# Loading a weight megabyte behind the first keys, with a new issue list for the repeated pass

## The chip, the core and the metric

The kernel runs on one core of a Trainium2 chip. Its engines work from queues of their own, each in the order in which its instructions were written: TensorE (PE, with PEld for its weight loads), VectorE (DVE), ScalarE (ACT), GpSimd (POOL), and SyncE (SP), which here only issues DMAs. The metric is the device time of one execution in microseconds, the median over several executions.

## The reference

Eight batches, 8 heads, 576 positions, head dimension 64. Keys and values are averaged over groups of 8 positions, softmax attention runs over the 72 pooled positions, and a gated block follows:

```python
scores = scale * np.matmul(q, k_p.transpose(0, 1, 3, 2))      # k_p: mean of 8 keys
attn = softmax(scores); x = attn @ v_p                        # heads side by side: [8, 576, 512]
h = gelu(x @ w_in)                                            # w_in [512, 1024], 8-byte numbers
u, v = h[..., :512], h[..., 512:]
v_n = (v - mean(v)) / sqrt(var(v) + 1e-6) * g_ln
v_s = einsum('ts,bsd->btd', w_sg, v_n) + b_sg                 # w_sg [576, 576]
out = x + (u * v_s) @ w_out
```

## The kernel before

The work of a batch is cut into steps, each a Python generator that issues some instructions and stops; each stop waits for its next turn. An entry `S3+1` in a list gives one more turn to step S, part 3, of the batch one ahead of the current one; a lower-case entry is work on weights (`lv0` loads a megabyte of the value half of w_in, `v0` gives a turn to the rebuilding of its first 128 rows, `d0` issues two matmuls on a block of zeros). Four lists are played: PROLOGUE (batch 0 and the weights), FIRST (around batch 1), PERIOD (played five times, for batches 2 to 6) and LAST (batch 7). All engines take their order from them, and nothing reorders it afterwards. An entry whose step is already finished issues nothing.

The steps that matter here, with their lines:

- A, B, C, E load keys, values, queries and the last eight pooled positions of a batch ("left"). `load` is line 222, and all of these go to SP's queue. SP has eight semaphores for its DMAs and uses them in turn, so its ninth DMA waits until the first has landed, the tenth for the second, and so on.
- `v0`, `v1` turn the 8-byte numbers of w_in into 4-byte ones: two ACT instructions (lines 263 and 267), two DVE (269, 270), one POOL (272), then a rounded part by ACT (275) and a rest by POOL (277).
- K pools the keys. In batch 0 PE does it (tiles kvraw and bbc), ACT copies the result (tile kp, 419), DVE pools the left positions (lp, 407), PE transposes kp and lp (445, 447), and ACT writes the scaled key block kbd (459, 460).
- Q transposes the queries (530) and ACT copies them into qbuf (533). S multiplies qbuf by kbd for the scores (a group of kbd,qbuf matmuls), DVE finds the maxima (557), ACT the exponentials (576; in batch 0, 571), DVE the reciprocals (593, 594) and the product (597).
- s transposes w_sg in five pieces (303), each split by ACT (225, 310) and DVE (227, 312).
- H is the value half of x @ w_in (5 parts), with normalisation on DVE (762, 763, 768) and POOL (765, 766). U is the other half, W the multiplication by w_sg (matmuls wsh,vk), with DVE (833, 835) behind it. V, G and O are attention times values, sums for a seven-product multiplication, and the product with w_out. P pools the values (vp, 407).

PSUM is four double banks that are handed around in the order in which they were given back. A step that takes a bank waits for the last reader of the step that gave that bank back.

Of the kernel before, what the change touches and what calls it, by code (L numbers as in the profile page):

```python
# [20 lines left out]


PROLOGUE = """
d0 lv0 d0 A1+0 A0+0 E0+0 v0 d0 E1+0 C0+0 d0 d0 v1 v0 C1+0 K2+0 d0 d0 v1 d0 K1+0 K1+0 K0+0 K0+0 K2+0 P2+0 Q0+0 K2+0
Q1+0 Q0+0 S0+0 v0 S0+0 C2+0 S0+0 Q2+0 Q1+0 v0 v1 lv1 v1 S1+0 S1+0 v0 C3+0 Q2+0 S2+0 S1+0 S2+0 v1 ls0 S0+0 Q3+0 S0+0
B0+0 B1+0 S1+0 Q3+0 S2+0 S0+0 A1+1 S0+0 S2+0 S3+0 S1+0 v3 s2 S2+0 S0+0 S0+0 T0+0 s2 T0+0 S3+0 S2+0 v3 S1+0 s1 S3+0
S1+0 v3 S2+0 s0 S3+0 s4 s2 S1+0 s1 s4 S3+0 s1 S3+0 A0+1 lu0 S3+0 s0 v2 S1+0 v3 S2+0 S3+0 P1+0 E0+1 s4 S2+0 s0 T1+0
# [20 lines left out]
O0+0 S2+0 Z3+0 Z0+0 Z2+0 Z3+0 V3+1 Z2+0  # L48
""".split()
PERIOD = """  # L50
V1+0 S0+1 S0+1 S0+1 H3+0 H3+0 H3+0 V0+0 H1+0 H2+0 V3+0 H0+0 H1+0 H1+0 H3+0 H2+0 H2+0 S1+1 H3+0 H1+0 V2+0 U0+0 H0+0
H1+0 H2+0 S1+1 H0+0 Q2+1 H2+0 H4+0 S1+1 C3+1 H0+0 Q3+1 H4+0 S1+1 U1+0 H0+0 H4+0 S3+1 H3+0 U0+0 S3+1 T0+1 H0+0 H4+0
H4+0 U1+0 S3+1 S2+1 P1+1 H4+0 T0+1 S1+1 C2+2 U3+0 A1+2 H1+0 T0+1 S2+1 H4+0 W0-4 S3+1 H2+0 P0+1 S2+1 H4+0 T0+1 S3+1
S2+1 W0+0 S2+1 T0+1 P2+1 W3+0 C0+2 A0+2 P2+1 L0+1 U3+0 P2+1 W0+0 P2+1 K1+2 W1+0 K0+2 U2+0 W1+0 L0+1 G0+0 W2+0 U2+0
W3+0 G1+0 T1+1 G1+0 L0+1 G0+0 L0+1 G1+0 L0+1 Q0+2 W2+0 T2+1 V0+1 G2+0 L0+1 O1+0 T1+1 T1+1 V1+1 E0+2 G2+0 V0+1 B0+2
G4+0 G2+0 T2+1 O0+0 K2+2 T2+1 V2+1 O0+0 G3+0 G2+0 V1+1 T3+1 G2+0 G3+0 W1-5 O0+0 G3+0 T3+1 V2+1 T3+1 V3+1 O0+0 B1+2
O0+0 G4+0 K2+2 O0+0 G4+0 O2+0 V0+1 O1+0 G4+0 K2+2 K2+2 C1+2 O1+0 O2+0 O1+0 K2+2 G4+0 S0+2 Z1+0 Z0+0 O0+0 S0+2 Z1+0
O0+0 Z3+0 V3+1 V1+1 Z0+0 V2+1 Q1+2 Z3+0 Z2+0 Z2+0 V3+1
""".split()
LAST = """  # L60
H1+0 H3+0 V2+0 V1+0 H1+0 H3+0 H1+0 H1+0 H2+0 H3+0 T3-7 H2+0 V0+0 H1+0 H2+0 H0+0 S0-2 V3+0 H4+0 H3+0 H4+0 H3+0 H2+0
# [1009 lines left out]
```

## Time and profile before

| | us |
|---|---|
| median of 3 runs (lowest, highest) | 556.76 (556.32, 559.84) |
| profiled execution | 555.78 |
| its span, first to last instruction | 553.8 |
| TensorE busy in the span | 540.8 |
| VectorE, ScalarE, GpSimd busy | 393.7, 375.9, 358.9 |

The profiled execution is 1.98 us longer than its span, and 0.98 us below the median of the runs. TensorE's granted clock is 0.999 of the full one over the span. Times inside the span are counted from its first instruction; the five passes over PERIOD lie between about 161 and 482 us.

### The profile page before, as it was taken

The numbers are of one execution on the slowest core, as the hardware profiler recorded it, in microseconds if no ns is written. First come the engines' busy times: TensorE is split into PE (matmuls) and PEld (weight loads), VectorE is DVE, ScalarE is ACT, GpSimd is POOL, SyncE is SP. The second block draws the span as 40 slices with busy tenths as digits, with TensorE's granted clock in tenths as the row PEclk, the third lists the DMA queues.
The fourth block names the chain that finished last, engine by engine and source line by source line (L and its number), as shares of the span: only waits on it lengthen the run. The fifth ranks groups of instructions, "written<-read, shape, count | busy, mean of one in ns | idle before, by whom it ended". The sixth has DMA issues, their size and how long they took to land.

```text
span 553.8 us, 10591 instructions
## 1 busy us (share of the span) xinstructions
PE 540.8 (98%) x3665; PEld 505.8 (91%) x3665; DVE 393.7 (71%) x562; ACT 375.9 (68%) x986; POOL 358.9 (65%) x415
## 2 busy tenths in 40 slices
PE   8899999999999999999999999999999999999996
PEld 7688799988999899989999899998999899998996
DVE  5999999767646778567976779567886677455164
ACT  4699658986274897678866696866966798643220
POOL 5578786988788257944589246963489437892440
PEclk9999999999999999999999999999999999999999
DMA  9989723672341644444552725436362530004005
GB/s 249 335 193 255 215 53 71 129 138 45 78 82 18 119 91 127 79 68 83 131 117 35 128 44 136 99 57 118 82 161 39 90 61 12 12 14 73 1 1 86
DMA packets 204197, 54.33 MB, mean 98 GB/s; under 512 B 185904, under 2 KB 191664, under 8 KB 204144
## 3 DMA queue, kind: packets, MB, share of 16 engines
q1 hardware_dynamic: 199280, 53.07, 45.1%
q10 hardware_dynamic: 4864, 0.59, 0.7%
q8 instruction: 29, 0.48, 0.4%
q14 instruction: 24, 0.20, 0.1%
HBM read 40.21 MB, written 13.42 MB: 97 GB/s over the span
## 4 chain that ended last, share of the span: by engine, by line
PE 79%; DVE 8%; DMA 4%; ACT 3%; issue 2%; POOL 2%; SPq 1%; DVEq 0%; POOLq 0%; ACTq 0%
PE ps L134 78%; DMA left<-in_moe_w_sg 2%; SPq L222 1%; DVE xmem L921 1%; PE ps L170 1%; DMA kvraw<-in_k 1%; DVE al L689 1%; DMA far<-e 1%; DVE ps L833 1%; DVE umem L835 1%; ACT ah L682 1%; ACT gk L849 1%; PE ps L303 0%; DVE e L567 0%; DVE vp L407 0%
## 5 line engine op out<-in xcount | busy, mean ns | idle before, releaser
L134 PE MATMUL ps<-wsh,vk 128*128 128x288 f32 x512 | 97.1, 296 | 0.1
L134 PE MATMUL ps<-xhlk,wih 128*128 128x288 f32 x512 | 90.3, 298 | 1.5 <-DVE e L597 0.7
L134 PE MATMUL ps<-wih,xhlk 128*128 128x512 f32 x256 | 83.5, 398 | 0.3 <-DVE e L597 0.2
L134 PEld LDWEIGHTS ps<-wsh,vk 128*128 128x128 f32 x512 | 78.2, 188 | 1.3 <-DVE left L768 1.3
L134 PEld LDWEIGHTS ps<-xhlk,wih 128*128 128x128 f32 x512 | 75.4, 188 | 3.2 <-PE ps L134 0.9
L576 ACT ACTIVATE e<-ps,nmax 128x72 f32<-128x72 f32 x240 | 73.0, 336 | 6.5 <-DVE nmax L557 2.5
L134 PEld LDWEIGHTS ps<-wih,xhlk 128*128 128x128 f32 x256 | 48.1, 188 | 12.2 <-DVE e L597 0.5
L134 PE MATMUL ps<-wsl,vk 128*128 128x288 f32 x256 | 57.4, 295 | 0.0
L134 PE MATMUL ps<-xhlk,wil 128*128 128x288 f32 x256 | 55.1, 296 | 0.0
L576 ACT ACTIVATION_READ_ACCUMULATOR e<-ps,nmax 128x1 f32 x240 | 53.4, 223 | 0.0
L134 PE MATMUL ps<-wil,xhlk 128*128 128x512 f32 x128 | 50.6, 395 | 0.0
L774 POOL TENSOR_TENSOR vk<-xmem,vk 128x512 fp32r<-128x512 f32 x32 | 40.9, 1290 | 14.6 <-ACT vk L772 14.5
L605 POOL COPY el<-e 128x40 f32<-128x40 f32 x64 | 12.8, 254 | 53.8 <-issue 22.3
L921 DVE TENSOR_TENSOR xmem<-ps,xmem 128x576 f32<-128x576 f32 x42 | 31.5, 751 | 22.8 <-PE ps L134 22.4
L721 POOL TENSOR_TENSOR xhlk<-xmem,xhlk 128x576 fp32r<-128x576 f32 x32 | 45.2, 1434 | 1.4 <-ACT xhlk L719 1.4
L134 PE MATMUL ps<-gk,woh 128*128 128x288 f32 x224 | 46.1, 297 | 0.0
L134 PE MATMUL ps<-kbd,qbuf 128*128 128x144 f32 x320 | 44.2, 288 | 1.5 <-ACT qbuf L533 1.0
L134 PEld LDWEIGHTS ps<-kbd,qbuf 128*128 128x128 f32 x320 | 41.4, 190 | 3.7 <-ACT qbuf L533 1.4
L134 PEld LDWEIGHTS ps<-wsl,vk 128*128 128x128 f32 x256 | 42.2, 188 | 0.0
L134 PEld LDWEIGHTS ps<-xhlk,wil 128*128 128x128 f32 x256 | 41.0, 188 | 0.0
L865 POOL TENSOR_TENSOR umem<-umem 128x576 f32<-128x576 f32 x24 | 34.4, 1432 | 8.2 <-issue 6.9
L833 DVE SCALAR_TENSOR_TENSOR ps<-ps,gcol,bbc 128x576 f32<-128x576 f32 x28 | 22.9, 820 | 22.5 <-PE ps L134 22.3
(198 smaller groups left out, 1424.3 us busy)
## 6 DMA issues: line engine op xcount, KB each, us to landing
kvraw<-in_k SPq DMA_DIRECT2D x32, 256.0 KB
qbuf<-in_q SPq DMA_DIRECT2D x112, 72.0 KB
out<-umem SPq DMA_DIRECT2D x112, 72.0 KB
kvraw<-in_v SPq DMA_DIRECT2D x28, 256.0 KB
vraw<-in_moe_w_in SPq DMA_DIRECT2D x2, 1024.0 KB
graw<-in_moe_w_in SPq DMA_DIRECT2D x2, 1024.0 KB
eraw<-far SPq DMA_DIRECT2D x28, 72.0 KB
far<-e SPq DMA_DIRECT2D x7, 256.0 KB
```

Source lines behind the costliest of these rows:

```text
L134: nc.tensor.matmul(o, lhsT, rhs, start=start, stop=stop, **flags)
L170: nc.tensor.transpose(ps[:rows, i * P:(i + 1) * P], src(i), ident if i < NT - 1 else swap)
L222: queue.dma_start(o, i)
L576: nc.scalar.activation(e[:, i, h], slots[i][:, h], AF.Exp, bias=nmax[:, i, h:h + 1], **acc)
L605: nc.gpsimd.tensor_copy(st["el", b].rearrange("p t (n j a) -> p t n j a", n=2, a=4)[:, :, g // 2, :, 2 * (g % 2) + h], ef[:, :, LEFT[h]:LE ...
L682: nc.scalar.copy(ah, ps[:, 0:S])
L689: nc.vector.tensor_tensor(al, ps[:, 0:S], ah.bitcast(F32), op=ALU.subtract)
L721: nc.gpsimd.tensor_tensor(xhl[:, 1, g], x32[:, g], xhl[:, 0, g].bitcast(F32), op=ALU.subtract)
L774: nc.gpsimd.tensor_tensor(lo, vg, hi.bitcast(F32), op=ALU.subtract)
L833: nc.vector.scalar_tensor_tensor(vs, vs, gcol[:, d:d + 1], bbc.rearrange("p (a n) -> p a n", a=2), op0=ALU.mult, op1=ALU.add)
L865: nc.gpsimd.tensor_tensor(x, p, q, op=ALU.subtract)
L921: nc.vector.tensor_tensor(x, ps[:, :, 0:HALF], x, op=ALU.add)
```

## The change

In PROLOGUE the entry `lv0` moves from the second place to behind `A1+0 A0+0`, the loads of the keys of batch 0. The entries of PERIOD are the same 172 as before in another order. FIRST, LAST and the rest of PROLOGUE are not touched, and no instruction is added or removed.

```diff
 PROLOGUE = """
-d0 lv0 d0 A1+0 A0+0 E0+0 v0 d0 E1+0 C0+0 d0 d0 v1 v0 C1+0 K2+0 d0 d0 v1 d0 K1+0 K1+0 K0+0 K0+0 K2+0 P2+0 Q0+0 K2+0
+d0 d0 A1+0 A0+0 lv0 E0+0 v0 d0 E1+0 C0+0 d0 d0 v1 v0 C1+0 K2+0 d0 d0 v1 d0 K1+0 K1+0 K0+0 K0+0 K2+0 P2+0 Q0+0 K2+0
...
 PERIOD = """
-V1+0 S0+1 S0+1 S0+1 H3+0 H3+0 H3+0 V0+0 H1+0 H2+0 V3+0 H0+0 H1+0 H1+0 H3+0 H2+0 H2+0 S1+1 H3+0 H1+0 V2+0 U0+0 H0+0
...
+H2+0 S0+1 H3+0 V3+0 H1+0 H2+0 V1+0 S0+1 H3+0 H2+0 V0+0 H1+0 H3+0 V2+0 H0+0 H2+0 H1+0 H3+0 C3+1 S1+1 H4+0 H1+0 H2+0
...
```

SP's queue at the start of the program is the one place where the first edit shows; the other four engines keep their order up to the first pass over PERIOD. Here kvraw<-in_k are the keys of batch 0, vraw the megabyte of w_in, and left the last eight positions:

```order
 L1067 UNCONDITIONAL_BRANCH
+L222 DMA kvraw<-in_k 128x1x512 x4
 L222 DMA vraw<-in_moe_w_in 128x2x1024
-L222 DMA kvraw<-in_k 128x1x512 x4
 L222 DMA left<-in_k 32x1x512 x2
 L222 DMA left<-in_v 32x1x512 x2
```

The four DMAs of keys pass the one of w_in; what follows keeps its place.

DVE in the second pass over PERIOD, from the maxima of the third set of scores (S3) on, before. ps_3047 and ps_3081 are the banks of S3 and S2, ps_2989 that of H4, the last part of H:

```order
L557 TENSOR_REDUCE nmax_3055<-ps_3047 128x10
L762 BN_STATS bst_3061<-ps_2989 64x6
L763 BN_AGGR mv_3062<-bst_3061 64x2
L407 TENSOR_REDUCE vp_3087<-kvraw_2731 128x128
L768 TENSOR_SCALAR left_120<-ps_2989,mv_3062,rstd_3065 64x512
L665 STREAM_TRANSPOSE eraw_110<-eraw_110 128x576
L557 TENSOR_REDUCE nmax_3130<-ps_3081 128x10
L593 TENSOR_SCALAR ps_3047<-ssum_3070 128x5x2
L594 RECIPROCAL ps_3047<-ps_3047 128x5x2
L597 TENSOR_TENSOR e_3069<-e_3069,ps_3047 128x720
L407 TENSOR_REDUCE vp_3087<-kvraw_2657 128x128
```

And the same stretch in the change, where ps_3061 is the bank of S3, ps_3076 that of S2 and ps_2950 that of H4:

```order
L557 TENSOR_REDUCE nmax_3067<-ps_3061 128x10
L762 BN_STATS bst_3069<-ps_2950 64x6
L763 BN_AGGR mv_3070<-bst_3069 64x2
L768 TENSOR_SCALAR left_120<-ps_2950,mv_3070,rstd_3073 64x512
L539 STREAM_TRANSPOSE qbuf_111<-qbuf_111 128x576
L557 TENSOR_REDUCE nmax_3085<-ps_3076 128x10
L407 TENSOR_REDUCE vp_2995<-kvraw_2757 128x128
L593 TENSOR_SCALAR ps_3061<-ssum_3088 128x5x2
L594 RECIPROCAL ps_3061<-ps_3061 128x5x2
L597 TENSOR_TENSOR e_3087<-e_3087,ps_3061 128x720
```

The pooling of the values (L407) that stood ahead of H4's last reader (L768) now stands ahead of the reciprocals of S3; of the other moves on DVE, a query transposition (L539) comes forward and the transposition of eraw (L665) goes back. On PE, H4 passes the first U, and the W parts come in the order 1, 0, 3, 2 where they came as 0, 3, 1, 2. The first W takes H4's bank and the second W S3's bank, before and after.

## Rows read from the trace of the kernel before

**Rows 1.** The page: span, TensorE's busy time, DMA rate in 40 slices.
```profile
span 553.8 us, 10591 instructions
...
PE 540.8 (98%) x3665; PEld 505.8 (91%) x3665; DVE 393.7 (71%) x562; ACT 375.9 (68%) x986; POOL 358.9 (65%) x415
...
GB/s 249 335 193 255 215 53 71 129 138 45 78 82 18 119 91 127 79 68 83 131 117 35 128 44 136 99 57 118 82 161 39 90 61 12 12 14 73 1 1 86
```

**Rows 2.** Stretches: start:end, length, each engine's busy time, clock, DMA share, GB/s.
```profile
290.00:353.90 63.90, 63.78 (x435) 60.14 (x435) 47.43 (x66) 48.16 (x139) 40.57 (x46) 1.00 0.47 93
```

**Rows 3.** SP's issues in order of time: start, us, DMA, count.
```profile
0.73 0.46 SPq L222 DMA_DIRECT2D vraw<-in_moe_w_in  x1
1.25 2.62 SPq L222 DMA_DIRECT2D kvraw<-in_k  x4
```

**Rows 4.** Chain of work that ended last, at the start: start, us, what.
```profile
3.27 6.04 DMA kvraw<-in_k
...
15.17 8.45 DMA left<-in_moe_w_sg
```

**Rows 5.** TensorE in order of time: start, us, group, [idle before, releaser].
```profile
7.53 3.94 PE L134 MATMUL ps<-kvraw,bbc 128*128 128x128 f32 x32
...
12.09 0.27 PE L447 MATMUL ps<-ident,lp 128*128 128x128 f32 x1
...
14.05 1.49 PE L134 MATMUL ps<-kbd,qbuf 128*128 128x144 f32 x10
```

**Rows 6.** ScalarE in order of time.
```profile
5.68 0.67 ACT L263 ACTIVATE tops<-vraw 128x512 f32<-128x512 f32 x1 [3.67 <-DMA vraw<-in_moe_w_in]
...
7.40 0.66 ACT L267 ACTIVATE vraw<-vraw 128x512 int32<-128x512 uint32 x1
...
11.50 0.27 ACT L419 COPY kp<-ps 128x128 f32<-128x128 f32 x1 [1.72 <-PE ps L134]
12.40 0.38 ACT L459 ACTIVATE kbd<-ps 64x256 f32<-64x256 f32 x1 [0.64 <-PE ps L447]
```

**Rows 7.** VectorE in order of time.
```profile
6.38 0.43 DVE L269 TENSOR_SCALAR tops<-tops 128x512 int32<-128x512 int32 x1 [3.64 <-ACT tops L263]
6.84 0.69 DVE L270 SCALAR_TENSOR_TENSOR tops<-vraw,tops 128x512 int32<-128x512 int32 x1
...
9.45 1.93 DVE L407 TENSOR_REDUCE lp<-left 32x128 f32<-32x1024 f32 x1 [1.92 <-DMA left<-in_k]
...
15.58 0.91 DVE L557 TENSOR_REDUCE nmax<-ps 128x10 f32<-128x720 f32 x1 [0.47 <-PE ps L134]
...
41.64 0.91 DVE L557 TENSOR_REDUCE nmax<-ps 128x10 f32<-128x720 f32 x1 [1.35 <-PE ps L134]
```

**Rows 8.** All engines in order of time, around 29 us.
```profile
29.46 0.20 PEld L303 LDWEIGHTS ps<-ident,umem 128*128 128x128 f32 x2 [0.15 <-DVE wtl L312]
```

**Rows 9.** VectorE in order of time, in one pass over PERIOD.
```profile
328.97 1.98 DVE L407 TENSOR_REDUCE vp<-kvraw 128x128 f32<-128x1024 f32 x1
330.88 0.79 DVE L768 TENSOR_SCALAR left<-ps,mv,rstd 64x512 f32<-64x512 f32 x1
331.59 0.76 DVE L665 STREAM_TRANSPOSE eraw<-eraw 128x576 f32<-128x576 f32 x1
332.29 0.86 DVE L557 TENSOR_REDUCE nmax<-ps 128x10 f32<-128x720 f32 x1
...
333.52 0.90 DVE L597 TENSOR_TENSOR e<-e,ps 128x720 f32<-128x720 f32 x1
334.34 2.02 DVE L407 TENSOR_REDUCE vp<-kvraw 128x128 f32<-128x1024 f32 x1
```

**Rows 10.** GpSimd in the same pass.
```profile
329.38 0.54 POOL L766 TENSOR_TENSOR rstd<-rstd,mhalf 64x1 f32<-64x1 f32 x1
```

**Rows 11.** TensorE's weight loads in the same pass.
```profile
331.72 0.30 PEld L134 LDWEIGHTS ps<-wsh,vk 128*128 128x128 f32 x2 [0.25 <-DVE left L768]
...
335.43 0.33 PEld L134 LDWEIGHTS ps<-wsh,vk 128*128 128x128 f32 x2
```

More of the change, by code (lines that the diff above doesn't have):

```diff
@@ L50 @@
 PERIOD = """
-V1+0 S0+1 S0+1 S0+1 H3+0 H3+0 H3+0 V0+0 H1+0 H2+0 V3+0 H0+0 H1+0 H1+0 H3+0 H2+0 H2+0 S1+1 H3+0 H1+0 V2+0 U0+0 H0+0
[L52 to L58, printed above, removed]
+H2+0 S0+1 H3+0 V3+0 H1+0 H2+0 V1+0 S0+1 H3+0 H2+0 V0+0 H1+0 H3+0 V2+0 H0+0 H2+0 H1+0 H3+0 C3+1 S1+1 H4+0 H1+0 H2+0
+W1-5 H0+0 S1+1 S0+1 C0+2 H0+0 Q3+1 H3+0 H1+0 S1+1 H3+0 W0-4 H0+0 P1+1 U1+0 H2+0 H0+0 S1+1 H4+0 H0+0 H4+0 U0+0 T0+1
+U1+0 H4+0 Q2+1 U0+0 S3+1 S3+1 H4+0 S2+1 H4+0 H1+0 Q0+2 S2+1 S3+1 H4+0 P0+1 T0+1 S2+1 H4+0 A1+2 U3+0 S3+1 T0+1 U3+0
+W1+0 S1+1 S2+1 S3+1 A0+2 K1+2 P2+1 S2+1 C2+2 W0+0 P2+1 W0+0 W3+0 T0+1 L0+1 W1+0 K0+2 U2+0 W3+0 G0+0 T0+1 G1+0 P2+1
+G0+0 W2+0 U2+0 P2+1 G1+0 L0+1 L0+1 E0+2 G1+0 L0+1 T2+1 W2+0 L0+1 G2+0 T1+1 V0+1 O0+0 T1+1 C1+2 V0+1 T1+1 L0+1 G2+0
+V1+1 K2+2 G2+0 G4+0 T2+1 G3+0 G2+0 T2+1 O1+0 V1+1 G2+0 O0+0 G3+0 V2+1 T3+1 O0+0 T3+1 G3+0 T3+1 G4+0 O0+0 K2+2 V3+1
+B1+2 K2+2 O0+0 G4+0 O0+0 V2+1 B0+2 O1+0 V3+1 K2+2 V1+1 G4+0 K2+2 O2+0 O2+0 G4+0 O1+0 O1+0 V0+1 S0+2 V2+1 Z1+0 V3+1
+Z1+0 S0+2 Z0+0 O0+0 Q1+2 Z0+0 O0+0 Z3+0 Z2+0 Z3+0 Z2+0
 """.split()
```

## The prediction

> **What bounds the kernel now.** I read the page first: TensorE is busy for 540.8 of 553.8 us, 98% [rows 1]. Only 13.0 us of the span are without a matmul, which is the most that a change of order alone could give back. The stretch table says where they are not: in one pass over PERIOD TensorE is busy for 63.78 of 63.90 us while VectorE has 47.43, ScalarE 48.16 and GpSimd 40.57 [rows 2]. A pass is bound by TensorE's own instructions, and a new order of the same instructions can win tenths of a microsecond in it. It can lose more, because every step hands on one of four PSUM banks and each of the other engines works in order.
>
> The start is bound by something else. The chain of waits begins with SP's issues and the landing of the keys at 9.31 (3.27 + 6.04), goes through SP's next issues, and ends on the landing of the last piece of w_sg at 23.62 [rows 4]. On TensorE, though, the pooling of the keys starts at 7.53 with no idle time before it, straight behind the matmuls on zeros, and runs for 3.94 us in one piece [rows 5]. VectorE is what I followed next: from its first maximum at 15.58 to 41.6 its timeline shows no wait worth listing; the next is 1.35 us at 41.64, for TensorE [rows 7]. And TensorE waits for VectorE at 29.46, when a bank comes free behind a subtraction of w_sg [rows 8]. So whatever makes VectorE late at 15.58 arrives at TensorE at 29.46, and from there TensorE is the one that is late.
>
> **First edit: the megabyte behind the keys.** It removes and adds nothing; five DMAs change places on SP's queue. Four issues of keys take 2.62 us together, so they go from 0.73 to 3.35 instead of 1.25 to 3.87 [rows 3], and the weight issue of 0.46 ends at 3.8. Nothing behind them on SP moves in order, and the lanes that the later issues wait for are the same in number.
>
> *What the keys gain.* Nothing that I can price above 0.1 us: their pooling on TensorE starts at 7.53 behind the matmuls on zeros, which wait for no load, and shows no idle time [rows 5].
>
> *What the weights lose.* They landed just before 5.68, where ScalarE takes them up after 3.67 us of waiting [rows 6]. Now they are the last of the same two megabytes. The last of those two landed at 9.31 [rows 4], with its issue ending at 3.87; the weights' issue would end at 3.8. I take 9.31. The lower bound is 2.1 MB at the second slice's 335 GB/s [rows 1], 6.3 us from 1.2, so 7.5. The row of the same queue with the same bytes ahead is the nearer one.
>
> *Who is queued behind them.* ScalarE: `v0` and `v1` are four instructions, of which the first starts at 5.68 and the last at 7.40 and takes 0.66 [rows 6], so 2.38 us for all. They would run from 9.33 to 11.71, and the two copies of the pooled keys, 0.27 each, follow: the second ends at some 12.2 instead of 11.77. VectorE: lines 269 and 270 of `v0` stand ahead of the pooling of the left keys (lp). Line 269 starts with the end of ScalarE's first instruction, 9.33 + 0.67 = 10.0; line 270 comes 0.46 later and takes 0.69 [rows 7], so lp starts at 11.2 where it started at 9.45. It is 1.75 us late, and ends at 13.1.
>
> *Who waits for that.* TensorE's transposition of lp, at 12.09 [rows 5], moves to 13.15; kbd, which ScalarE begins at 12.40 when that is done [rows 6], is 1.05 late, and so are the first scores, which now begin at 15.1 and end at 16.6. VectorE has its own work in between and had 0.47 us of idle time before its first maximum [rows 7]; that absorbs a part: 1.75 - 0.47 = 1.28 us. The maximum comes at 16.86, behind both. From there nothing on VectorE gives before 41.6, and TensorE takes it over at 29.46. **Term: +1.3 us**, between 0 (weights landed by 7.5: 7.5 + 1.9 = 9.4, when the left keys land anyway) and +1.75 (nothing absorbed). Less than nothing is excluded but for the 0.1 above, since w_sg, the next to be waited for, lands behind the same bytes as before.
>
> **Second edit: the order in PERIOD.** Its end is nearly the same list (two places where VectorE's results are just in time keep their order on all engines), and in its first half the margins are above 0.3 us as I add them up. What changes is the handover to the four W steps. Before, the first W waits 0.25 us for H4's bank [rows 11], because VectorE pools values (1.98 us) ahead of H4's last reader, at 330.88 [rows 9]. GpSimd's factor for that reader is there at 329.92 [rows 10]. In the change it follows at once: 329.95, so the bank is free at 330.7 and the first W doesn't wait. **-0.25 us.** But the second W takes S3's bank, and its last reader (line 597) now stands behind a query transposition, the maxima of S2 and the other pooling of values. With the rows' steps [rows 9]: 329.95 + 0.71 (line 768) + 0.70 (a transposition, by the one at 331.59) + 1.23 (maxima and the two small ones, 332.29 to 333.52) + 2.02 = 334.61, and 0.90 for the product: 335.51. Unhindered the second W would now load its weights at 335.43 - 0.25 = 335.18 [rows 11], so it waits 0.33 us. The two cancel within 0.1 us; I take **0** for each of five passes, with bounds of -0.25 (no second wait) and +0.25 (the second wait half a microsecond), so -1.3 to +1.3 for all. The moved query transposition needs its load, and the moved loads wait on SP for S1's matmuls, but these lie ten microseconds ahead; the eraw transposition that goes back is read 15 us later. I cost both at nothing; if one of them came late, VectorE would hold S3's bank, which is a rival below.
>
> **The sum.** 555.78 for the profiled execution, + 1.3 + 0 = 557.1; by the median of the runs, 556.76 + 1.3 = 558.06, so **558.0**.
>
> **Rivals.** *The weights land early.* The transfers ahead of them may pack better with keys first. The first megabyte alone needed 0.73 to 5.66, 4.93 us; the same from an issue at 3.35 ends at 8.3, lp starts at 10.2, 0.75 late, of which 0.47 are absorbed: +0.3, time 557.0. For it: the DMA rate rises from 249 to 335 GB/s in the second slice [rows 1]. Against it: the keys, as last of the two megabytes, needed until 9.31. In the Trainium skill, "DMA: Bandwidth & Descriptors" (Anatomy of one DMA) gives a fixed 2.0 us plus the bytes at 436 GB/s for one DMA of GpSimd's path; by that, as an estimate, a megabyte issued at 3.4 lands at 7.8 and the term is 0, time 556.8. The 4.93 us measured here for a lone first megabyte is longer than its 4.4.
>
> *The new list is better than my sum.* The first W's wait goes and the second has none: -1.3 over five passes, with the first term 557 - 0.2 = 556.8, without it 555.5. For it: the wait of 0.25 stands in the trace; against it: VectorE's order as written.
>
> *VectorE is held in every pass: slower.* The pooling of values that ran at 334.34 [rows 9] now runs at 332.6, ahead of S3's reciprocals. If its load, or the query load in front of it, is not there, VectorE stands, S3's bank stays taken and TensorE waits from 335.2 on, microsecond for microsecond, five times. Held for 1.1 us more than I add up it costs 1%; at 1.5 us, 7.5 us in all, time 565.5. For it: the reciprocals lose their place ahead of a 2 us reduction. Against it: before, that reduction shows no wait either, and VectorE has 16 us to spare in a pass [rows 2].
>
> **How the numbers follow.** Forecast 0.48; weights early 0.25; list better 0.18; VectorE held 0.07; a gain of over 1%, 5.6 us, would need nearly half of all idle time of TensorE, 0.02. A measurement of this kernel tells some 1% from no change. The range reaches from 555.2 (both gains, and 0.3 for the runs' spread) to 560.4 (1.75 + 1.3, and 0.6 for the spread); it leaves out the held VectorE beyond 1% and the large gain. Faster by over 1% 0.02, within 1% 0.91, slower by over 1% 0.07.
>
> **What would show it.** In the changed profile: ScalarE's line 263 waiting for the weights until about 9.3; lp at 11.2, the first scores at 15.1, VectorE's first maximum at 16.9; TensorE's wait at 29.46 longer by about a microsecond, and the stretch up to 97.3 longer by 1.3. In each pass no wait before the first W and one of some 0.3 before the second, a length of 63.9 as before. It is wrong if lp is not late, if the delay is gone by 41.6, or if a pass changes by more than 0.25 us.

## The result and the profile after

The changed kernel takes 563.81 us in the median of six runs (563.06 to 564.33), the kernel before 556.73 (555.42 to 559.84) beside it: a ratio of 1.0123, with an interval of 1.0097 to 1.0149. It is slower by 7.1 us; the forecast was +1.3, with an upper end of +3.6. The profiled execution took 564.33 us, 8.55 more than the one before.

The page: span, busy time, DMA rate in 40 slices, against [rows 1].

```profile
span 562.1 us, 10595 instructions
...
PE 542.2 (96%) x3665; PEld 507.6 (90%) x3665; DVE 393.8 (70%) x562; ACT 375.0 (67%) x986; POOL 359.7 (64%) x415
...
GB/s 198 279 229 225 258 63 100 81 151 64 78 91 1 98 110 90 66 92 118 92 84 102 92 115 79 52 105 111 79 95 119 76 77 12 12 7 79 1 1 85
```

TensorE's busy time has grown by 1.4 us only; the rest of the 8.3 us of span is idle time. The first two slices move 198 and 279 GB/s where they moved 249 and 335: the loads at the start are the first place to look. Three engines at the start, in order of time, against [rows 5], [rows 6] and [rows 7]; first ScalarE, then VectorE, then TensorE:

```profile
13.49 0.66 ACT L263 ACTIVATE tops<-vraw 128x512 f32<-128x512 f32 x1 [11.49 <-DMA vraw<-in_moe_w_in]
...
17.92 0.38 ACT L459 ACTIVATE kbd<-ps 64x256 f32<-64x256 f32 x1 [1.79 <-PE ps L447]
```

```profile
14.19 0.43 DVE L269 TENSOR_SCALAR tops<-tops 128x512 int32<-128x512 int32 x1 [11.45 <-ACT tops L263]
...
15.37 1.92 DVE L407 TENSOR_REDUCE lp<-left 32x128 f32<-32x1024 f32 x1
...
20.72 0.28 DVE L405 TENSOR_TENSOR lp<-left 32x128 f32<-32x128 f32 x1
22.38 0.91 DVE L557 TENSOR_REDUCE nmax<-ps 128x10 f32<-128x720 f32 x1 [1.37 <-PE ps L134]
```

```profile
6.99 3.74 PE L134 MATMUL ps<-kvraw,bbc 128*128 128x128 f32 x32
16.19 0.69 PE L445 MATMUL ps<-ident,kp 128*128 128x128 f32 x2 [5.47 <-ACT kp L419]
17.44 0.45 PE L447 MATMUL ps<-ident,lp 128*128 128x128 f32 x1 [0.56 <-DVE lp L407]
17.68 2.13 PE L530 MATMUL ps<-ident,early 96*128 96x96 f32 x12
19.60 2.74 PE L134 MATMUL ps<-kbd,qbuf 128*128 128x144 f32 x10
```

The order of the waits is the predicted one, and the sizes are not. ScalarE takes up the weights at 13.49, 7.81 us later than before. VectorE had 1.92 us to spare there, since it waited for the left keys anyway; lp is 5.92 late. L447 is 5.35 late and the first scores start 5.55 late. Then ten score matmuls take 2.74 us where they took 1.49, so the first maximum is 6.80 late. TensorE meanwhile stands for 5.47 us, at a place where it stood for 0.36 before, and comes back slower. That row of the kernel before:

```profile
11.82 0.44 PE L445 MATMUL ps<-ident,kp 128*128 128x128 f32 x2 [0.36 <-ACT kp L419]
```

The stretches of the change show it by the granted clock (first number: length; the last three: clock, DMA share, GB/s):

```profile
11.00:16.00 5.00, 0.00 (x0) 0.00 (x0) 1.75 (x3) 2.51 (x6) 0.52 (x1) 0.96 0.75 144
16.00:20.00 4.00, 3.25 (x17) 2.82 (x18) 3.87 (x5) 1.85 (x7) 2.16 (x2) 0.50 0.99 289
20.00:24.00 4.00, 4.00 (x26) 3.94 (x25) 2.49 (x4) 2.15 (x4) 2.83 (x3) 0.70 1.11 297
```

From 16 to 20 the clock is 0.50, the lower of its two levels (1.2 of 2.4 GHz); by 24 it is back. At the first matmul of attention times values around 161 us the delay is 6.9 us:

```profile
167.94 0.40 PE L134 MATMUL ps<-ah,vbh 128*128 128x288 f32 x1 [0.51 <-DVE al L689]
```

In the kernel before, the same matmul with the same wait stands at 161.06:

```profile
161.06 0.40 PE L134 MATMUL ps<-ah,vbh 128*128 128x288 f32 x1 [0.51 <-DVE al L689]
```

The other 1.4 us come in the passes over PERIOD. One pass, from the first W to the next, by its busy times (columns as in [rows 2]) and by what TensorE's matmuls waited for (total, times, longest):

```profile
275.44:339.64 64.20, 63.80 (x437) 60.16 (x436) 47.50 (x67) 48.68 (x143) 40.72 (x45) 1.00 0.45 93
```

```profile
PE ps L134 <- DVE al L689: 0.2, 1, 0.2
PE ps L134 <- DVE e L597: 0.2, 1, 0.2
```

The same pass in the kernel before, from 267.81 to 331.72, is 63.91 long with 63.77 busy, and the list of its waits has neither of these two rows: what TensorE waits there ahead of its matmuls is below 0.07 us each time. The change is 0.29 us longer: 0.16 at the second W (the predicted wait for line 597) and some 0.12 more at the wait for line 689.

### The profile page after: what moved, and what is told of

Read it like the earlier page. It is cut to its first block, busy times and chain, and to the rows that moved or that the text cites. A ratio compares the mean times of both kernels' runs of the same rounds, so it can differ in the third digit from the quotient of the medians.

```text
span 562.1 us, 10595 instructions
## 1 busy us (share of the span) xinstructions
PE 542.2 (96%) x3665; PEld 507.6 (90%) x3665; DVE 393.8 (70%) x562; ACT 375.0 (67%) x986; POOL 359.7 (64%) x415
## 5 line engine op out<-in xcount | busy, mean ns | idle before, releaser
L765 POOL TENSOR_TENSOR rstd<-mv,eps 128x1 f32<-128x1 f32 (+1 forms) x40 | 7.6, 189 | 87.1 <-DVE mv L763 86.9
L134 PEld LDWEIGHTS ps<-wih,xhlk 128*128 128x128 f32 x256 | 48.1, 188 | 12.2 <-ACT gk L723 0.5
L134 PE MATMUL ps<-kbd,qbuf 128*128 128x144 f32 x320 | 45.5, 293 | 1.5 <-ACT qbuf L533 1.1
L134 PEld LDWEIGHTS ps<-kbd,qbuf 128*128 128x128 f32 x320 | 42.6, 194 | 3.6 <-ACT qbuf L533 1.3
```

The costliest lines, as they stand in the source:

```text
L134: nc.tensor.matmul(o, lhsT, rhs, start=start, stop=stop, **flags)
L765: nc.gpsimd.tensor_tensor(rstd, mv[:, 1:2], eps[:n, 1:2], op=ALU.add)
```

## The experiments

Every run goes against the kernel before on the same chip. The ratio is worked out from the single runs and is not quite that of the two medians. The table has the results but for e5 and e6, which ran once each, and of which only the profile is read.

| run | edit | us, before | ratio (interval) |
|---|---|---|---|
| e1 | first edit alone | 562.25, 557.05 | 1.0087 (1.0064, 1.0111) |
| e2 | second edit alone | 558.76, 557.05 | 1.0034 (1.0018, 1.0051) |
| e3 | e1, first turns of v0, v1 later | 568.71, 557.05 | 1.0206 (1.0184, 1.0227) |
| e4 | e1, queries in larger pieces | 563.09, 557.05 | 1.0104 (1.0078, 1.0130) |
| e7 | e2, P0 moved back | 557.52, 557.96 | 0.9998 (0.9981, 1.0015) |
| e8 | two keys, weights, two keys | 563.06, 557.96 | 1.0078 (1.0046, 1.0110) |
| e9 | before, weights in four DMAs | 558.95, 556.96 | 1.0031 (1.0014, 1.0048) |
| e10 | e1, keys in two DMAs | 560.45, 556.96 | 1.0063 (1.0039, 1.0087) |
| e11 | before, keys in two DMAs | 558.79, 557.69 | 1.0017 (0.9994, 1.0039) |
| e12 | e11 and e7 | 557.03, 557.69 | 0.9995 (0.9978, 1.0013) |
| e13 | e1, TensorE kept busy, many banks | 568.76, 557.34 | 1.0203 (1.0167, 1.0240) |
| e14 | the same in one bank | 563.78, 557.34 | 1.0103 (1.0069, 1.0137) |
| e15 | e14 with half the matmuls | 562.05, 557.13 | 1.0072 (1.0047, 1.0097) |

### Each edit alone

e1 has PROLOGUE of the change and PERIOD of before, e2 the reverse.

> Only the first edit: PROLOGUE of the change, PERIOD of the kernel before. The changed kernel's profiled execution was 8.55 us longer than the one before, of which I read 6.9 us ahead of the first pass over PERIOD and the rest inside the passes. If the two edits add up, this kernel is 6.9 us slower than the one before (563.6, 563.0 to 564.4), its megabyte of w_in lands at about 13.5 and VectorE's first maximum starts at about 22.4. Rival: the late landing at 13.5 was an accident of the executions shown, and the weights land near the 9.31 that I had taken; then the time is 558 (557 to 559).

> Only the second edit: PROLOGUE of the kernel before, PERIOD of the change. The prediction gave it 0 (a wait of 0.25 us goes at the first W, one of 0.33 comes at the second): 556.8. The trace of the change has passes of 64.25 us where they were 63.9 to 64.1, so some 0.25 to 0.3 us more in each: 558.1 (557.6 to 558.6), with the weights landing at 5.66 as before. Rival: those passes were longer only because they started late, with another phase against the loads; then this kernel is within 0.4 us of the one before.

The medians are 5.2 and 1.7 us above the kernel before, 6.9 together, and the change measured 7.1: the two add up. The weights landed at 13.32 in e1's profile (564.3, the slowest of its four runs) and the first maximum came at 22.22, so the late landing is no accident, though its size varies: with the same loads in the same order it was 12.20 to 14.41 in the profiles of e1, e13, e14, e15 and the change. Counted from first W to first W, passes took 63.93, 63.92, 64.30 and 63.93 us in e1 and 64.38, 64.19, 64.43 and 64.20 in e2, so their length goes with the list and not with the start.

One thing has to be kept out of these comparisons. The kernel before, too, has executions in which TensorE's clock was low for some time at the start: beside e1 and e2 its mean granted clock is 0.998 or more in 15 of 17 runs, with a median of 556.96, and 0.995 and 0.997 in the other two, which took 558.80 and 558.85. All six runs of the change have 0.993 or 0.994, so there the low clock belongs to the kernel. In e2 it is 0.997 or less in 5 of 12 runs, its profiled one among them, which is already 3.55 us late at the first pass (207.43 for 203.88) although its start is that of before. Its other seven runs have a median of 558.20, 1.2 above the 556.96, and its four passes are 1.35 us longer together.

### Where the 1.7 us of the second edit are

e7 moves one entry of e2's PERIOD:

```diff
-H4+0 P0+1 T0+1 S2+1 H4+0 A1+2 U3+0 S3+1 T0+1 U3+0
+H4+0 T0+1 S2+1 H4+0 A1+2 U3+0 S3+1 P0+1 T0+1 U3+0
```

> Only the second edit, with one entry moved back: the pooling of values P0 stands behind the reciprocals and the product of S3 instead of ahead of them. In the kernel with the new PERIOD alone a pass takes 64.2 to 64.4 us against 63.92, with a wait of 0.17 us for line 597 ahead of the second W and one of 0.18 for line 689 further on. Theory, the pooling ahead of S3's reciprocals costs it: the first of the two waits goes, a pass takes 64.05 to 64.15, and the time is 0.8 us below that kernel: 558.0 against a median of 557.05 for the kernel before. If the wait for line 689 comes from the same delay, that goes too, a pass takes 63.9 and the time is 557.0. Rival: the extra time is in the changed order of the first half of the pass, and a pass stays at 64.2 or more.

One pass each of e2 and of e7, and TensorE's longer waits in that of e2 (the trace in order of time):

```profile
271.81:336.00 64.19, 63.80 (x438) 60.17 (x436) 47.50 (x67) 48.76 (x144) 40.82 (x45) 1.00 0.46 93
```

```profile
275.87 0.50 PE L134 MATMUL ps<-wsh,vk 128*128 128x288 f32 x2 [0.16 <-DVE e L597]
297.18 0.40 PE L134 MATMUL ps<-ah,vbh 128*128 128x288 f32 x1 [0.17 <-DVE al L689]
```

```profile
268.70:332.51 63.81, 63.56 (x437) 60.13 (x436) 47.42 (x67) 48.77 (x143) 40.61 (x45) 1.00 0.47 94
```

With P0 back, the wait ahead of the second W is gone and the pass is 0.38 us shorter, more than the wait itself (the busy time falls as well); the wait for line 689 stays at 0.19. The four passes take 64.27, 63.81, 63.85 and 63.81, the first still with a wait for line 597. The pooling of values ahead of S3's reciprocals was what the new list lost by; mended, it is level with the old one, not better.

### Who hands the delay on

e3 takes the weights' consumers out of the way of the keys:

```diff
-... lv0 E0+0 v0 d0 E1+0 C0+0 d0 d0 v1 v0 C1+0 K2+0 d0 d0 v1 d0 ... S0+0 v0 S0+0 C2+0 S0+0 Q2+0 Q1+0 v0 v1 lv1 v1
+... lv0 E0+0 d0 E1+0 C0+0 d0 d0 C1+0 K2+0 d0 d0 d0 ... S0+0 S0+0 C2+0 S0+0 v0 v1 v0 v1 Q2+0 Q1+0 v0 v0 v1 lv1 v1
```

> The first edit alone, and the first two turns each of v0 and v1 (ScalarE's lines 263 and 267, VectorE's 269 and 270) moved behind the maximum and the exponentials of S0, so that neither engine stands at the weights with the keys' work behind it. Theory in-order queues: the whole loss comes from ScalarE and VectorE standing there; the first maximum is back at 15.6 or earlier and the time at that of the kernel before, 556.8 (556 to 557.8). Rival, the queue of SP: the fourth load of queries still waits until 13.5 for the semaphore of the weights, so lv1, w_sg and the values are issued 4 us late as in the change; ScalarE and VectorE then stand at the second queries or at w_sg instead, and 3 to 5 us of the 6.9 stay: 560 to 562.

It went the other way from both: 11.7 us slower. Its TensorE at the start, then SP's issue of the fourth load of queries and what SP waited for between 8 and 15 us:

```profile
11.16 0.44 PE L445 MATMUL ps<-ident,kp 128*128 128x128 f32 x2 [0.36 <-ACT kp L419]
13.08 0.30 PE L447 MATMUL ps<-ident,lp 128*128 128x128 f32 x1 [1.48 <-DVE lp L407]
14.51 0.69 PE L530 MATMUL ps<-ident,early 96*128 96x96 f32 x6 [1.14 <-DMA early<-in_q]
16.16 1.19 PE L530 MATMUL ps<-ident,early 96*128 96x96 f32 x6 [0.96 <-DMA early<-in_q]
17.14 2.66 PE L134 MATMUL ps<-kbd,qbuf 128*128 128x144 f32 x10
```

```profile
13.49 0.31 SPq L222 DMA_DIRECT2D early<-in_q  x1
```

```profile
SPq L222 <- DMA vraw<-in_moe_w_in: 4.8, 1, 4.8
```

The keys' path no longer stands at the weights (kp at 11.16), but the queries are late in its place. SP issues the fourth of their loads at 13.49 (9.32 in the kernel before), when the weights have landed, because it uses the same semaphore, and the first scores wait behind the transposition of those queries. The first maximum came at 19.84, still 4.3 us late, 1.2 of them from scores at a low clock (2.66 us for 1.49). So the delay has two roads, ScalarE's and VectorE's queues (6.6 us at the first maximum of e1) and SP's queue with the loads behind the weights (4.3 us), and e3 closes the first. The rest of its loss comes later, where v0 and v1 now stand among the softmax work and TensorE's mean clock from 24 to 40 us is 0.68 (1.00 in e1). I take it to say nothing on the first edit.

### Why the weights land at 13.4

Four runs ask whether what follows the megabyte makes it late, or what goes ahead. e4 loads the queries in pieces of 1536 bytes instead of 256 (part of its output is then other numbers, at the same work), e6 puts queries and not left positions right behind the weights, e5 lets nothing follow until they have landed, and e8 puts two of the four loads of keys behind them. The lines that carry it:

```diff
+ load(early[0:S // 6, n + 6 * D * h:n + 6 * D * (h + 1)] if g < 3 else t[:, :, h], ...)            # e4
+ name == 'v' and j == 0 and load(fark[0][0:1, 0:64], raw[0:1, 0, 0:64].bitcast(F32))               # e5
- d0 d0 A1+0 A0+0 lv0 E0+0 v0 d0 E1+0 C0+0 d0 d0 v1 v0 C1+0 K2+0
+ d0 d0 A1+0 A0+0 lv0 v0 d0 C0+0 d0 d0 v1 v0 C1+0 E0+0 E1+0 K2+0                                     # e6
+ d0 d0 A1+0 lv0 A0+0 E0+0 v0 d0 E1+0 C0+0 d0 d0 v1 v0 C1+0 K2+0                                     # e8
```

> The first edit alone, with the six loads of queries into early done in pieces of 1536 bytes instead of 256 (same bytes and places in the queue; the positions of the first three pairs of heads of batch 0 are read in another order, so those outputs are of other numbers). Theory small pieces: the megabyte of weights lands late because the loads issued behind it, in pieces of 256 bytes, share the DMA engines with it; in large pieces they take less, the weights land at 10 or earlier, lp is at most 2.5 us late, of which 0.47 are absorbed, and the time is 558.8 (558 to 559.5). Rival: the weights are slow by themselves behind the keys; they land at about 13 as in the change, and the time stays at 563 (562 to 564).

> The first edit alone, with the four loads of left positions (64 KB each, into 32 partitions) moved behind the first four loads of queries, so that queries and not left positions follow the weights. Theory left loads: the megabyte is late because the loads into 32 partitions, issued right behind it, crowd it; it then lands two or more us earlier than 13.3, by 11. Rival, any follower does it: it lands at 13 to 14 as before, with queries in the place of the left positions. The time isn't compared, since the left positions come later than the keys need them.

> The first edit alone, with one small DMA behind the megabyte on SP's queue that reads its first row (256 bytes, into a scratch array that is overwritten later). SP waits for the weights to land before it issues that, so nothing of what follows (left positions, queries) is in flight beside the megabyte. Theory shared engines: the loads issued behind it made it late; alone behind the keys it lands at 8.5 to 9.5, 2.1 MB at the rate seen before. Rival: the megabyte is slow by itself behind four loads of keys; it lands at 12 or later again. The time isn't compared, since all later loads are held too.

> The first edit by half: two of the four loads of keys ahead of the megabyte, two behind. If the weights fall behind in proportion to the bytes ahead of them, they land at about 9.5 (halfway between 5.66 and 13.4), the keys behind them at 9 to 10; lp starts at 11.4, 1.9 late, and the time is 1.5 to 2.5 us above the kernel before: 558.5 to 559.5. Rival: what counts is what stands behind the megabyte, not ahead of it; two loads of keys shield it from the small loads, it lands at 7 (5.66 and the 1.3 of two key loads), the pooling of the left keys starts at 9.45 as before, and the time is that of the kernel before within half a microsecond.

The weights were taken up at 13.16 in e4 and 13.74 in e6, so neither the small pieces nor the left positions alone are the cause. In e5 they were at 11.05:

```profile
11.05 0.66 ACT L263 ACTIVATE tops<-vraw 128x512 f32<-128x512 f32 x1 [9.04 <-DMA vraw<-in_moe_w_in]
```

What shares the DMA engines with them costs some 2.3 us, then (1.2 to 3.4 against the five profiles above; e5 is one run), and even alone they come 1.7 us after the 9.31 that I had taken. e8 was the surprise: with only two loads of keys ahead the weights were there at 11.55, the last keys later still (ScalarE waited for their pooling until 17.33), and the first maximum came at 23.04. Neither of the two theories had that.

The DMA view of the first 12 us shows what happens (40 slices of 0.3 us; first the busy share of the 16 DMA engines in tenths, then GB/s), here before and e5:

```profile
DMA  0000009357999999999999999858999999999999
GB/s 0 0 0 0 0 0 205 68 137 300 396 437 437 410 396 403 382 410 382 369 369 417 389 410 410 328 225 261 260 263 228 212 221 203 158 172 223 194 220 207
```

```profile
DMA  0000000596979897488598598998754443200000
GB/s 0 0 0 0 0 0 0 109 164 232 369 280 416 280 266 294 178 314 266 205 239 266 218 294 300 355 335 328 287 218 191 191 178 123 96 0 0 0 0 1
```

Before, from 3.0 to 7.5 us, some 400 GB/s without a gap. In e5 the rate swings between 178 and 416 from the start, and in the last three microseconds before 10.5 the busy share falls step by step from 9 to 2 tenths. In the Trainium skill, "DMA: Bandwidth & Descriptors" (Why a DMA increments its semaphore by 16 and not by 1) says that a DMA runs on up to 16 engines that finish independently, each adding one to its semaphore, and counts as landed with the last. The falling share agrees, and so do the times at which the 16 steps of a DMA's semaphore came, which the trace records also have. For the weights they lie between 5.22 and 5.66 in the kernel before, between 8.43 and 11.03 in e5, and between 8.47 and 13.47 in the change. The last load of keys in the kernel before, from whose landing the forecast took its 9.31, had its first step at 8.10. So the first engine is done nearly when it should be, and the whole lateness lies between the first engine and the last.

The 7.8 us that the prediction estimated from another figure of that page of the Trainium skill fit no run with the keys first.

The trace's records of single DMA pieces show where the engines fall apart. The table counts pieces of 2 or 4 KB that took over 0.40 us (0.08 and 0.16 are usual) and began between 3 and 8 us, and gives the time by which the first megabyte of such pieces had moved, the time at which both megabytes, keys and weights, had landed, and the time from the first to the last step of the weights' semaphore:

```
                                            long pieces   first MB    landed       first to last step
1 MB of weights first: before, e2, e7       1, 0, 3       5.1-5.2     9.1-9.8      0.4-0.6
1 MB of weights first: e11, e12             0, 0          5.2         8.6, 8.9     0.3, 0.5
keys in two of 512 KB first: e10            3             5.6         10.4         2.1
weights in four of 256 KB first: e9         19            6.5         10.7         1.3-2.1 each
keys in four of 256 KB first: change, e1    20, 11        6.0, 6.1    13.5, 13.3   5.0, 4.6
  the same: e3, e4, e6, e13, e14, e15       10 to 18      6.0-6.6     12.2-14.4    3.1-5.5
  the same, nothing behind until 11: e5     17            6.3         11.0         2.6
two of 256 KB first: e8                     22            7.1         13.4         3.9
```

Wherever DMAs of 256 KB stand first, there are ten or more long pieces, and the steps lie apart. One reading of it, the theory of the backlog, is that the engines have drained each small DMA by the time SP has issued the next, and get out of step. e9 and e10 were made to test it: weights first but in small DMAs, and keys first but in large ones.

```diff
+ [load(raw[:, c, 512 * h:512 * h + 512], sv[:, c, 512 * h:512 * h + 512]) for c in range(2) for h in range(2)] if ...   # e9
+ load(t, sv[:, 0:JM].rearrange("h j l x -> j l h x")) if ...                                                    # e10
```

> The kernel before, with its first megabyte of w_in loaded by four DMAs of 256 KB (128 x 512, pieces of 2 KB, the shape of the loads of keys) instead of one; the order of the loads is that of before. Theory backlog: what slows the start is that the first DMAs are small, each drained as fast as SP issues the next, so that the DMA engines stand at the head of each DMA and get out of step; then this kernel starts badly too, with many pieces that take over 0.4 us up to 12 us (the kernel before has 9, the change 28), weights complete at 6.5 or later, the last keys after 10.5, and the time is 2 to 4 us longer (559 to 561). Rival source: reading in_k first is what is slow; then the weights land at about 5.7, the keys as before, and the time stays within 0.7 us of the kernel before.

> The first edit alone, with the keys loaded by two DMAs of 512 KB instead of four of 256 KB, same bytes, pieces of 2 KB. Theory backlog: SP has issued the keys and the megabyte by 2.1 instead of 4.0, so the DMA engines never run dry, the long pieces become few, the weights land at 9 to 10.5 instead of 13.3, and the time is 1.3 to 3 us above the kernel before (558.3 to 560). Rival source: nothing changes but the number of issues; the weights land at 12.5 or later and the time stays at 562 to 563.

In the loads both came out by that theory. In e10 the rate is whole again behind the start:

```profile
GB/s 0 0 0 0 0 0 0 75 184 96 177 321 416 423 403 396 410 437 403 382 355 369 369 396 423 369 396 278 240 205 241 238 202 201 230 178 113 102 155 239
```

```profile
10.41 0.66 ACT L263 ACTIVATE tops<-vraw 128x512 f32<-128x512 f32 x1 [8.41 <-DMA vraw<-in_moe_w_in]
```

Its weights land 3 us earlier than in e1, and it is 3.5 us above the kernel before instead of 5.2 (expected were 1.3 to 3). e9, with the kernel before's own order, lost 2.0 us (expected were 2 to 4): TensorE's pooling of the keys, which had waited for no load, waited 1.33 us for them.

```profile
9.22 3.81 PE L134 MATMUL ps<-kvraw,bbc 128*128 128x128 f32 x32 [1.33 <-DMA kvraw<-in_k]
```

It is the size of the first DMAs, then, and not their source; nor is it the size of the pieces, which are 2 KB for the keys of e10 and of e1 alike. It is not all: e10 takes away 2.9 of the 4.0 us between the landing in e1 (13.3) and that of the keys before (9.3), and the rest is open. That the DMA engines run dry between issues fits the rows, since SP needed 2.62 us for four issues of 256 KB [rows 3], which is 400 GB/s, the rate at which the engines drain. The steps of the semaphores show when each engine is done and not what held it up, so that part is argued.

### The clock, and a version with both mended

e13, e14 and e15 put matmuls on zeros into TensorE's stand ahead of the transposition of kp; the loads stay.

```diff
-K1+0 K1+0 K0+0 K0+0 K2+0 P2+0 Q0+0 K2+0
+K1+0 K1+0 K0+0 K0+0 d1 K2+0 P2+0 Q0+0 K2+0        # e14: d1 is 80 instructions in one bank; e15: 40; e13: 20 times d0
```

> The first edit alone, with 40 more matmuls on zeros on TensorE between the pooling of the keys and the transposition of kp, so that it is busy during most of the 5.5 us in which it stood for the late weights (in the changed kernel its granted clock behind that stand was 0.50 from 16 to 20 and 0.70 from 20 to 24, and ten score matmuls took 2.74 us instead of 1.49, twelve transpositions 2.13 instead of 1.35). Theory, the low clock is a part of the loss: the clock stays at 1.00, the scores take 1.49 again, VectorE's first maximum comes some 1.3 to 2 us earlier than 22.2 and the time is 1.3 to 2 us below that of the first edit alone, 560.3 to 561 where that had 562.25 (against 557.05 for the kernel before). Rival, it is not: VectorE's own late work sets the first maximum (its chain ended at 21.0 in the changed kernel), so at most 0.5 us return, and the matmuls on zeros that run too long can cost as much.

> As the run before, but all 40 matmuls on zeros go into one PSUM bank. In the run before 8 of them ran, the rest waited for the two banks that ScalarE's copies of the pooled keys still held, and 36 ran behind the weights at half the clock; so it filled nothing. Now they can run from 10.7 to 15.7, when TensorE has nothing else. Theory, the low clock is a part of the loss: the clock is 1.00 behind the stand, the way from the transposition of kp (16.0 to 16.2) to VectorE's first maximum takes 3.7 to 4.3 us (3.76 in the kernel before, 6.19 in the change), and the time is 1.3 to 2 us below the first edit alone, 560.3 to 561. Rival: the maximum stays at 21.5 or later behind VectorE's own work, and the time within 0.7 us of the first edit alone.

> As the run before with half as many matmuls on zeros. There one call was two instructions, so 80 ran, from 11.23 to 20.33, and TensorE came to the transposition of kp at 20.16, 4 us after the pooled keys were there; the way from it to VectorE's first maximum was 3.71 us at a clock of 1.00, against 6.2 with the stand. 40 instructions of 0.114 us take 4.6 us and end at about 15.6. Theory, the low clock is a part of the loss: the first maximum comes at 20.0 to 20.8 (22.2 with the stand), the time is 1.3 to 2.2 us below the first edit alone: 5.2 above the kernel before becomes 3 to 3.9. Rival: VectorE's own late work (its chain ends at 20.9 with the weights at 13.4) or the late queries take the place of the clock; the maximum is at 21.0 or later and less than 1.2 us return.

None of the three times came out by the theory. e13's matmuls waited for PSUM banks behind the weights, and e14's ran until 20.2, 4 us too long. e15's ended at 15.7, while the weights, at 14.41 in its profiled execution, kept TensorE standing until 17.12 after all, and the clock fell again:

```profile
17.12 0.44 PE L445 MATMUL ps<-ident,kp 128*128 128x128 f32 x2 [1.42 <-ACT kp L419]
```

```profile
20.00:24.00 4.00, 3.64 (x19) 3.63 (x20) 3.56 (x4) 2.06 (x5) 3.82 (x3) 0.57 1.12 326
```

Its time (1.0072) is near that of e1 (1.0087), as its rival had it. What e14 does show is the way behind the stand (TensorE, then VectorE, then the clock):

```profile
20.16 0.38 PE L445 MATMUL ps<-ident,kp 128*128 128x128 f32 x2
...
22.34 1.49 PE L134 MATMUL ps<-kbd,qbuf 128*128 128x144 f32 x10 [0.69 <-ACT qbuf L533]
```

```profile
23.87 0.91 DVE L557 TENSOR_REDUCE nmax<-ps 128x10 f32<-128x720 f32 x1 [2.43 <-PE ps L134]
```

```profile
20.00:24.00 4.00, 3.31 (x32) 3.12 (x32) 1.46 (x3) 3.14 (x8) 1.34 (x2) 1.00 1.14 239
```

From kp's transposition to the first maximum it is 3.71 us at a clock of 1.00 (3.76 before), and 6.19 in the change, of which 0.56 are a wait for lp. So the low clock costs TensorE's way 1.9 us. Not all of that counts at the first maximum: in the change VectorE has its own work until 21.00 (20.72 + 0.28), and only the 1.37 us that it then waits for TensorE can be the clock's. The 6.8 us are 5.4 from VectorE's late queue and 1.4 from the clock.

In the time of the whole kernel less came back. Only the profiled execution of e15 had the low clock (0.995 over the span). The other four kept 0.998 to 1.000 and took 561.2 to 563.0 us, while e1's four, at 0.994 to 0.997, took 561.4 to 564.3. The median of those four is 4.5 us above the kernel before, for e1's 5.2, and the ranges overlap. So a kept clock gave back little, and how much is open.

e11 and e12 try for a better kernel, with the weights first and the keys in two DMAs, e12 with e7's PERIOD too.

> The kernel before, with the weights first, and the four loads of keys of batch 0 done as two DMAs of 512 KB. Theory backlog: behind a whole megabyte the number of key DMAs is nearly indifferent to the DMA engines, which have work queued either way; SP is done with the keys some 1.2 us earlier, so the left positions and queries are queued earlier, lp starts up to 0.5 us before 9.45 and the time is 0 to 0.6 us shorter than before. Rival: larger key DMAs land later as a whole, the pooling of the keys on TensorE waits for them at 7.5, and the time is 0.5 to 1.5 us longer.

> The same loads, with the new PERIOD in which P0 is moved back behind the reciprocals of S3. In the run with that PERIOD alone four of five passes took 63.81 to 63.86 us against 63.92 (64.10 once) in the kernel before, and the first 64.27. If both parts add up, this is 0 to 0.8 us faster than the kernel before; if the first pass's extra 0.35 outweighs the rest, it is level with the run of the loads alone.

Neither can be told from the kernel before. lp begins at 9.50 in e11, as before, for its left keys land no earlier.

## Why the prediction was wrong

**The landing of the weights: wrong, and it decides.** The step that failed is "I take 9.31", with "The row of the same queue with the same bytes ahead is the nearer one". It takes the order of two megabytes to be indifferent for when both have moved. The runs show 13.32 to 13.49 in its place. When DMAs of 256 KB stand first the engines fall apart: the first is done with the weights at 8.47 and the last at 13.47. Even with nothing behind it the megabyte lands at 11.05 (e5), and the loads behind take some 2.3 us more; with the weights themselves in DMAs of 256 KB, both megabytes have landed at 10.7 instead of 9.3 (e9). The bounds, 7.5 to 9.31, came from rows in which a megabyte stood first, and so had no row for the other case; the upper one should have been open.

**Who is queued behind: right.** With 13.49 put into the prediction's own chain lp starts at 13.49 + 0.67 + 0.46 + 0.69 = 15.31; measured 15.37. No other wait was needed for it.

**Who waits for that: right, but without the clock.** "First scores at 15.1", 1.05 late, would be 5.2 late for this landing; measured 5.55. By its own sum for VectorE, lp's lateness less the 0.47 us that were free, the first maximum would be 5.92 - 0.47 = 5.45 late; measured 6.80, and the difference is nearly the 1.37 us that VectorE waits for the slow scores. The prediction let the matmuls keep their durations, while after a stand of 5.5 us the clock was 0.50: 2.74 us for 1.49. It had also named only the engines' queues. SP's fourth load of queries, at 13.49 in e3, is a second road that it did not see: "Nothing behind them on SP moves in order" is true of the order, and the semaphore that this load waits for is now that of a late DMA.

**From there to the end: right.** 6.80 us at the first maximum are 6.9 at 161 us; nothing was absorbed.

**The second edit: the handover was seen, the balance was wrong.** The second W waits for line 597 as predicted, 0.16 for 0.33. The failed step is "-0.25 us" for the first W. That wait stood on the weight loads [rows 11], while the pass had 0.12 us in all without a matmul [rows 2]: the load waited beside running matmuls, so there was at most 0.12 to gain. And the wait for line 689, in the end of the list that the prediction took to be nearly the same, grew by 0.12. The two don't cancel, a pass is 0.3 us longer, and all passes together cost 1.4 us in the changed kernel's profile, just beyond the upper bound of 1.3. The predicted rival "VectorE is held" did not come: the moved pooling waits for no load in the pass.

**The chances.** 0.91 for "within 1%" rested on the 9.31; the only rivals for the landing lay on the early side. The 0.07 for "slower by over 1%" was for a held VectorE, which is not what happened.

## What to carry to other kernels

When a load is moved behind others, its landing is not the last landing of before: look at what stands first on the queue, since behind small first DMAs the last of the 16 engines can be microseconds later than the first (5.0 us here, 0.4 behind nothing). Making the first DMAs larger took most of that away here. Follow a late load down every queue that will wait for it, the queue that shares its semaphore included, and look whether TensorE comes back from the stand at its lower clock. Compare runs by their granted clock too, since the kernel before lost it now and then by itself. A wait on the weight loads is a gain only as far as the matmul row has idle time beside it.

## What the runs showed of the hardware

- Two megabytes, keys and weights, had landed by 9.1 to 9.8 us with one DMA of 1 MB first (before, e2, e7), by 10.7 with that megabyte in four DMAs of 256 KB (e9), by 10.4 with the keys in two DMAs of 512 KB first (e10), and by 12.2 to 14.4 with the keys in four of 256 KB first (the change, e1, e3, e4, e6, e13 to e15).
- The 16 steps of the semaphore of a DMA of 1 MB came within 0.3 to 0.6 us when it stood first on the queue, and within 3.1 to 5.5 us behind four DMAs of 256 KB and with others behind it.
- The landing of a DMA behind small ones varies: 12.2 to 14.4 us in five profiles with the same loads.
- Behind 5.5 us without a matmul TensorE's granted clock was 0.50 from 16 to 20 us and 0.70 from 20 to 24. In e15's profiled execution, stands of 1.4, 0.8 and 0.6 us behind 4.6 us of matmuls on zeros were followed by 0.57 from 20 to 24; its other four executions kept 0.998 to 1.000 over the span.
